# A fused S4D and channel-MLP block: token set 1 of the first half prepared one slot later, and transposed by VectorE instead of TensorE

## The chip, the cores and the metric

The program runs on one core of a Trainium2 chip. The metric is the device time of one execution in microseconds (us). One execution was also recorded by the hardware profiler; its trace gives start and length of every instruction and DMA. TensorE is called PE here, VectorE DVE, ScalarE ACT, GpSimd POOL and SyncE SP. SP does no arithmetic: it issues DMAs, in the order of its program.

## The reference, cut to what matters

```python
# u: 1 x 2048 x 576 (L tokens, D features), w1: 576 x 4608, w2: 4608 x 576
x  = u
xn = layernorm(x)
s  = S4D(xn)                     # a long convolution over the tokens for each feature, with FFTs
y  = layernorm(xn)
g  = silu(gelu(y @ w1 + b1) @ w2 + b2)
out = x + s * g
```

The change is in the MLP branch, `y @ w1`, `gelu`, `@ w2`, and in how `y` gets to it. The convolution branch is interleaved with it on all engines.

## The kernel before, in words

**Tiles.** The 2048 tokens are 16 tiles of 128 tokens, in four sets of 512 (`TB`). The first half of the program does sets 0 and 1 of the MLP (tiles 0 to 7), the second half sets 2 and 3. Within a half the hidden dimension of 4608 is taken in `NG` = 12 groups of `G` = 3 blocks of 128. A group's weights are loaded from DRAM into the ring `raw`, split into a high part (ACT, `w1h`, `w2h`) and a rest (DVE, `w1l`, `w2l`), and used by two sets. Each of these weight tiles has one buffer.

**Slots.** A slot is one group for one set `tb`: `layer1` (three blocks of 14 matmuls with 512 columns into `mxa` or `mxb`), for each block gelu and its split into `hh` (ACT) and `hl` (DVE), and `layer2` (72 matmuls with 288 columns). The sum of `layer2` over the groups is kept in `acc`; DVE adds each of the four PSUM banks to it as it is finished, with the bias `bias2` in the first group. There are 48 slots. Slot 2n is group n for the half's first set, slot 2n+1 the same group for its second.

**The input of a set.** `layer1` needs the normalized tokens with features on the partitions: `XH` and `XL` (high part and rest of the first 512 features, as four blocks `kb`) and `XR` (the last 64). Each has room for two sets. In the first half tiles of a set are normalized by `second` into a `row` tile, transposed by PE (`y_transpose`, into the PSUM tiles `cv`) and split from PSUM by ACT and DVE. This is done for set 0 at the start and for set 1 (`turn_lines`) during slot 0. For the second half `second` stores the rows to DRAM (`y_s`); `block_lines` later loads them so that blocks of 32 tokens lie on 32 partitions (36 DMAs with pieces of 128 bytes), DVE transposes 32 x 32 blocks within them (`blocks`, L1236), and ACT and DVE split the result (`high`, `low`).

**Other work.** `params` loads four small tensors by 128-byte pieces (`kt`, `pr`, `mg`, `kt` again), transposes them on DVE (L688) and computes the parameters of the convolution. `x_load` of tiles 8 to 15 (eight DMAs of 288 KB, to `w` and `v`) is one step, `rest_of_norms`. PE's convolution work uses the PSUM tiles `cv`: `kgen` (L869, 36 times), `forward` (L941), `s2` (L979), `inverse` (L1032) and `i1` (L1059). A `kgen` can run alone between MLP matmuls, or be put directly ahead of another of these units (`ride`).

**What sets the order.** Each engine runs its instructions in the order in which the program lists them, and waits at the head of its list. The class `Order` makes that list: it keeps an estimated time for each engine, takes steps from many lines of steps as their inputs become ready by that estimate, and fixes the resulting order on each engine. A DMA has no engine in it: it is a step of some length without one (`step(None, 5.5, ...)`), listed on SP's queue at the moment when the planner takes it. `END`, `ALONE` and a margin in `pe_turns` decide when PE takes convolution units, and which `kgen` runs alone. Nearly all hardware DMAs are issued by SP.

Of the kernel before, what the change touches and what calls it, by code (L numbers as in the profile page):

```python
# [212 lines left out]
def mixer_kernel(ctx, tc, u, log_a_real, a_imag, c_real, c_imag, log_dt, d_skip, w1, b1, w2, b2,  # L213
# [22 lines left out]
    y_s = dr.tile([8, P, D], F32, name="y_s")  # L236
# [114 lines left out]
    def norms(b0, n):  # L351
# [31 lines left out]
        def second(t, engine=nc.vector):  # L383
            mv, rs = MV[b0]
            y = sb.tile([P, D], F32, name="row", bufs=NROW)
            engine.tensor_scalar(y, XT[b0 + t], mv[:, t, 0:1], rs[:, 1, t:t + 1], op0=OP.subtract, op1=OP.mult)  # L386
# [45 lines left out]
    for half in range(2):  # L432
        for g in range(NG):
            PARTS += [(half, g, 1, i) for i in range(KB + 1)] + [(half, g, 2, i) for i in range(G)]
# [3 lines left out]
    def load_raw(queue=nc.sync):  # L438
# [8 lines left out]
        if which == 2:  # L447
            queue.dma_start(r, w2[(g * G + i) * P:(g * G + i + 1) * P, :])
        elif i < KB:
            queue.dma_start(r, w1[i * P:(i + 1) * P, f])  # L450
        else:
            for e in range(2):
                queue.dma_start(r[e * 64:(e + 1) * 64], w1[KB * P:, f])
# [96 lines left out]
    def layer2(g, tb, j, terms, last, alone=False):  # L550
# [5 lines left out]
        c = slice(j * P, (j + 1) * P)  # L556
        if alone and terms[0][1]:
            Q2[j] = bank2("cv")
        elif j not in Q2:
            Q2[j] = bank2(mx(j + 1))  # L560
# [9 lines left out]
        def add(dh, n):  # L570
            o = acc[:, tb * 4 + j].rearrange("p (h d) -> p h d", h=2)[:, dh:dh + n]
            b = bias2.rearrange("p (h d) -> p h d", h=2)[:, dh:dh + n]
            nc.vector.tensor_add(o, q[:, dh:dh + n, :288], b if g == 0 else o)  # L573
# [616 lines left out]
    def norm_lines(b0, n=4):  # L1190
# [6 lines left out]
        for t in range(n):  # L1197
            nl["steps"].append(step("DVE", 0.6, lambda t=t: second(t), mark=("yn", b0 + t)))
            xl["steps"].append(step("POOL", 2.6, lambda t=t: first(t), need=[("yn", b0 + t)], mark=("xs", b0 + t)))
            wx["steps"].append(step(None, 5.0, lambda: None, need=[("xs", b0 + t)], mark=("xn", b0 + t)))  # L1200

    def turn_lines(b0, tb):
        x, xh, x2 = nl, nlh, nl2
        cell = {}

        def first(k0):
            for kb in (k0, k0 + 1):
                if kb <= KB:
                    cell[kb] = y_transpose(b0, tb, kb)
                    for i in range(4):  # L1210
                        cell[kb][0](i)
        M = lambda *a: ("turn", tb, b0) + a
        for ks in ((0, 1), (2, 3), (4,)):
            x["steps"].append(step("PE", 0.5 * len(ks), lambda k0=ks[0]: first(k0), cv=1,
                                   need=[M("l", 1)] if ks[0] == KB else (), mark=M("t", ks[0])))
            for kb in ks:
                xh["steps"].append(step("ACT", 0.6, lambda kb=kb: cell[kb][1](), need=[M("t", ks[0])], mark=M("h", kb)))
            for kb in ks:
                x2["steps"].append(step("DVE", 0.6, lambda kb=kb: cell[kb][2](), cv=-(kb == ks[-1]),
                                        need=[M("h", ks[-1])], mark=("x", tb) if kb == KB else M("l", kb)))  # L1220

    YB = []

    def block_lines():

        def load(tb, kb):
            if not YB:
                YB.extend(sb.tile([P, D], F32, name="row", bufs=NROW)[:, :TB] for _ in range(4))
            y = YB[(tb + kb) % 2]
            for q in range(4 if kb < KB else 2):  # L1230
                nc.sync.dma_start(y[32 * q:32 * q + 32].rearrange("p (b j) -> p b j", j=32), dram(
                    y_s, 4 * tb * P * D + kb * P + 32 * q, [[D, 32], [32 * D, NT], [1, 32]]))

        def blocks(tb, kb):
            n, k = P if kb < KB else 64, (tb + kb) % 2
            nc.vector.transpose(YB[2 + k][:n], YB[k][:n])  # L1236

        def high(tb, kb):
            y = YB[2 + (tb + kb) % 2]
            if kb < KB:  # L1240
                nc.scalar.activation(XH[:, kb, tb], y, AF.Copy)
            else:
                nc.scalar.activation(XR[:64, tb], y[:64], AF.Copy)

        def low(tb, kb):
            y = YB[2 + (tb + kb) % 2]
            if kb < KB:
                nc.vector.tensor_sub(XL[:, kb, tb], y, XH[:, kb, tb].bitcast(F32))
            else:
                nc.vector.tensor_sub(XR[64:, tb], y[:64], XR[:64, tb].bitcast(F32))  # L1250
        ks = [(tb, kb) for tb in range(2) for kb in range(KB + 1)]
        for n, k in enumerate(ks):
            yl["steps"].append(step(None, 5.5, lambda k=k: load(*k), need=[("yt",) + ks[n - 2]] if n > 1 else (), mark=("yl",) + k))
            ml["steps"].append(step("DVE", dve(TB), lambda k=k: blocks(*k), mark=("yt",) + k,
                                    need=[("yl",) + k] + ([("y2",) + ks[n - 2]] if n > 1 else [])))
            mlh["steps"].append(step("ACT", act(TB), lambda k=k: high(*k), need=[("yt",) + k, ("free", k[0])], mark=("yh",) + k))
            ml2["steps"].append(step("DVE", dve(TB), lambda k=k: low(*k), need=[("yh",) + k], mark=("y2",) + k))
# [43 lines left out]
    turn_lines(4, 1)  # L1301
# [4 lines left out]
    nl["steps"].append(step(None, 7.0, rest_of_norms))  # L1306
# [83 lines left out]
    later(mid - 2, G - 1, lambda: x_free(0))  # L1390
# [43 lines left out]
    for slot in range(NSLOT):  # L1434
        turn[0] = slot + 1
        g, tb = slot // 2 % NG, slot % 2
        n = slot // 2
        final = slot >= NSLOT - 2
        for pos in range(NPOS):
            if pos < G:  # L1440
                need = wmark(n, 1) + [("x", tb)]
                if pos == 0:
# [4 lines left out]
                    if slot in (1, 2 * NG + 1):  # L1447
# [11 lines left out]
                if pos == G - 1 and tb == 1 and slot + 1 < NSLOT:  # L1459
                    weigh_in(1)  # L1460
            else:
# [12 lines left out]
                if last or halves:  # L1474
# [10 lines left out]
                    elif g == NG - 1:  # L1485
# [5 lines left out]
                if pos == NPOS - 1 and tb == 1 and slot + 1 < NSLOT:  # L1491
# [4 lines left out]
            pe_turns(all_lines=pos in (0, 1, G + 1, G + 4, NPOS - 1))  # L1496
# [55 lines left out]
```

## Time and profile before

| | |
|---|---|
| time, median of 3 runs (lowest, highest) | 1083.9 us (1082.99, 1084.34) |
| the profiled execution's own time | 1082.74 us |
| its span, first to last instruction | 1081.0 us |
| granted TensorE clock | 0.998 |
| busy time of DVE, ACT, POOL | 947.9, 650.7, 199.1 us |
| moved by DMA | 125.54 MB, 116 GB/s on average |

The profiled execution is 1.2 us below the median. Times of single instructions count from the start of the span. A timeline row is: start, length, engine, line, operation, output<-inputs, shapes, count, and in brackets the engine's idle time before it and what ended it. "q" behind an engine is its queue: such a row issues a DMA, and its length is that of the issue; the landing of the data is given apart. Rows of one line without a gap are merged, so that their length is that of all of them. Matmuls overlap: the distance of their starts tells their cost, not their length.

### The profile page before, as it was taken

How to read it: one execution, taken by the hardware profiler on the slowest of the kernel's cores; microseconds unless marked ns; L12 is line 12 of the kernel's file. 1: busy time of each engine (PE TensorE's matmuls, PEld its weight loads, DVE VectorE, ACT ScalarE, POOL GpSimd, SP SyncE). 2: the span in 40 equal slices, each digit the busy share in tenths (PEclk: the TensorE clock that was granted, in tenths of full speed). 3: DMA queues.
4: the chain of work that ended last, by engine and by line, in shares of the span. 5: the costliest groups of instructions: out<-in, count | busy, mean ns of one | idle time of the engine just before them, and what ended most of it. 6: DMA issues, size and time to landing. Idle time of an engine off the chain costs nothing.

```text
span 1081.0 us, 27198 instructions
## 1 busy us (share of the span) xinstructions
PE 1071.7 (99%) x11491; PEld 933.9 (86%) x11491; DVE 947.9 (88%) x1518; ACT 650.7 (60%) x974; POOL 199.1 (18%) x281
## 2 busy tenths in 40 slices
PE   9999999999999999999999999999999999999997
PEld 7989999889888888888888888888888887888896
DVE  7797878989999999999999999999999996677366
ACT  6558569767666665767756666576665754233333
POOL 6559342110000200002100010000100022110231
PEclk9999999999999999999999999999999999999999
DMA  7746455823225221455523433142312347332344
GB/s 236 229 140 190 163 186 196 229 71 113 72 71 110 65 80 55 112 94 129 144 59 100 82 86 88 33 124 55 97 53 76 115 85 237 111 111 88 89 156 117
DMA packets 136537, 125.54 MB, mean 116 GB/s; under 512 B 88156, under 2 KB 108096, under 8 KB 135392
## 3 DMA queue, kind: packets, MB, share of 16 engines
q1 hardware_dynamic: 120624, 76.44, 26.2%
q0 software_dynamic: 15040, 46.40, 13.8%
q8 instruction: 90, 1.47, 0.6%
q10 hardware_dynamic: 752, 0.97, 0.3%
q14 instruction: 31, 0.25, 0.1%
HBM read 95.52 MB, written 34.01 MB: 120 GB/s over the span
## 4 chain that ended last, share of the span: by engine, by line
PE 98%; DVE 1%; issue 1%; DMA 0%; ACT 0%; POOL 0%; ACTq 0%; POOLq 0%; DVEq 0%
PE mxa L508 22%; PE mxa L565 21%; PE mxb L565 21%; PE mxb L508 21%; PE cv L869 3%; PE cv L979 3%; PE cv L1032 2%; PE cv L941 2%; PE cv L1059 1%; DMA idp<-in_ident_dram 0%; PE mxa L523 0%; PE cv L413 0%; DVE A L646 0%; DVE row L386 0%; DVE acc L573 0%
## 5 line engine op out<-in xcount | busy, mean ns | idle before, releaser
L565 PE MATMUL mxa<-w2h,hh 128*128 128x288 f32 x573 | 171.3, 299 | 0.0
L565 PE MATMUL mxb<-w2h,hh 128*128 128x288 f32 x576 | 170.9, 297 | 0.0
L565 PE MATMUL mxb<-w2h,hl 128*128 128x288 f32 x576 | 170.0, 295 | 0.0
L565 PE MATMUL mxb<-w2l,hh 128*128 128x288 f32 x576 | 169.6, 294 | 0.0
L565 PE MATMUL mxa<-w2h,hl 128*128 128x288 f32 x573 | 169.1, 295 | 0.0
L565 PE MATMUL mxa<-w2l,hh 128*128 128x288 f32 x573 | 168.7, 294 | 0.0
L547 DVE TENSOR_TENSOR hl<-h,hh 128x512 fp32r<-128x512 f32 x144 | 99.4, 692 | 76.8 <-ACT hh L544 76.1
L541 ACT ACTIVATE h<-mxa,b1t 128x512 f32<-128x512 f32 x73 | 50.2, 690 | 126.3 <-PE mxa L508 121.7
L769 POOL DMA_DIRECT2D par<-par_s x36 | 27.3, 759 | 519.4 <-DVE mg L812 479.7
L565 PEld LDWEIGHTS mxa<-w2h,hh 128*128 128x128 f32 x573 | 107.6, 188 | 9.4 <-issue 6.3
L565 PEld LDWEIGHTS mxb<-w2h,hh 128*128 128x128 f32 x576 | 108.2, 188 | 4.9 <-issue 2.5
L565 PEld LDWEIGHTS mxb<-w2l,hh 128*128 128x128 f32 x576 | 108.1, 188 | 0.6
L565 PEld LDWEIGHTS mxa<-w2l,hh 128*128 128x128 f32 x573 | 107.6, 188 | 0.7
L565 PEld LDWEIGHTS mxb<-w2h,hl 128*128 128x128 f32 x576 | 108.1, 188 | 0.0
L565 PEld LDWEIGHTS mxa<-w2h,hl 128*128 128x128 f32 x573 | 107.5, 188 | 0.0
L541 ACT ACTIVATE h<-mxb,b1t 128x512 f32<-128x512 f32 x71 | 48.9, 689 | 76.9 <-PE mxb L508 76.1
L544 ACT ACTIVATE hh<-h 128x512 fp32r<-128x512 f32 x144 | 90.8, 632 | 4.0
L573 DVE TENSOR_TENSOR acc<-mxa,acc 128x576 f32<-128x576 f32 x88 | 65.4, 743 | 17.0 <-PE mxa L565 16.7
L508 PE MATMUL mxa<-XH,w1h 128*128 128x512 f32 x284 | 80.2, 404 | 0.0
L508 PE MATMUL mxb<-XH,w1h 128*128 128x512 f32 x280 | 77.1, 397 | 0.0
L508 PE MATMUL mxa<-XL,w1h 128*128 128x512 f32 x284 | 76.2, 390 | 0.0
L508 PE MATMUL mxa<-XH,w1l 128*128 128x512 f32 x284 | 76.0, 389 | 0.0
(231 smaller groups left out, 2420.8 us busy)
## 6 DMA issues: line engine op xcount, KB each, us to landing
raw<-in_B_w_dram SPq DMA_DIRECT2D x72, 288.0 KB, 3.3
raw<-in_B_w_dram SPq DMA_DIRECT2D x96, 192.0 KB, 2.9
par_s<-A POOLq DMA_DIRECT2D x8, 1080.0 KB, 5.9
par<-par_s POOLq DMA_DIRECT2D x36, 240.0 KB, 3.3
f2t<-f2q SPq DMA_DIRECT2D x24, 256.0 KB, 3.7
raw<-in_B_w_dram SPq DMA_DIRECT2D x48, 96.0 KB, 3.6
u_s<-in_A_u_dram POOLq DMA_DIRECT2D x16, 288.0 KB, 4.3
xc<-xn_s SPq DMA_DIRECT2D x48, 96.0 KB, 3.8
```

The costliest lines, as they stand in the source:

```text
L508: nc.tensor.matmul(q, a, b, start=j == 0, stop=j == len(ops) - 1)
L541: nc.scalar.activation(t, q, AF.Gelu_apprx_tanh, bias=b1t[:, g * G + i:g * G + i + 1], scale=1.0)
L544: LAST[0] = nc.scalar.activation(hh[:, i], t, AF.Copy)
L547: nc.vector.tensor_sub(hl[:, i], t, hh[:, i].bitcast(F32))
L565: nc.tensor.matmul(q[:, dh, :288], a[:, i, c], b[:, i, d], start=i == 0 and k == 0, stop=i == G - 1 and k == 2)
L573: nc.vector.tensor_add(o, q[:, dh:dh + n, :288], b if g == 0 else o)
L769: nc.gpsimd.dma_start(PAR[b].rearrange("p (g i) k -> p g (i k)", g=4), dram(par_s, (b // 6 * CH + b % 6 * 4) * NPAR, [[D * NPAR, P], [24 * ...
L869: nc.tensor.matmul(q[32 * g:32 * g + 32, i // 2, i % 2 * 64:i % 2 * 64 + 64], U[:, ri, 4 * g + i, :], v[:, ri, 4 * g + i, :], start=ri == ...
L941: nc.tensor.matmul(Q1ST[i, x][g // 2][64 * f:64 * f + 64, g % 2].rearrange(order), f1t[r].rearrange("p s k -> p (s k)"), rhs(r, f), start= ...
L979: nc.tensor.matmul(Q[i][32 * q:32 * q + 32, f, 2 * ri:2 * ri + 2], m[r, 4 * i + q, 32 * ri:32 * ri + 32], A2[r, 4 * p + 2 * i + q // 2, :, ...
L1032: nc.tensor.matmul(QI[q // 2][64 * f:64 * f + 64, q % 2, i], MAT["g2t", p + i // 2][r, i % 2, ri], YS[p + i // 2][0][r, i % 2, ri, f], sta ...
L1059: nc.tensor.matmul(Q[f][32 * e:32 * e + 32, t], g1t[r], A2[r, k:k + 2, 1].rearrange("p i d r -> p i r d"), start=True, stop=True, skip_gro ...
```

## The change

Slots are no longer two for each group. Slot 0 is group 0 with set 0; slots 1 to 22 are groups 1 to 11 with sets 0 and 1; slot 23 is group 0 with set 1; slots 24 and 25 are group 0 with sets 2 and 3, with the same weights; then groups 1 to 11 follow. There are 24 loads of weights as before. Set 1 is thus first used in slot 2 instead of slot 1, and group 1's weights in slot 1 instead of slot 2.

Set 1's tiles 4 to 7 are no longer transposed by PE. `second` stores them to `y_s` (now 12 tiles); SP loads them back as four blocks of 128 tokens (16 DMAs of 64 KB, pieces of 512 bytes) and one of the last 64 features (2 DMAs, pieces of 128 bytes) into parts of `A2`; DVE transposes and ACT and DVE split as in the second half. Sets 2 and 3 use the same 512-byte form. For that the features are dealt out differently: block `kb` of `XH` holds features `4*p + kb` instead of `128*kb + p`, so that the rows of `w1` are loaded with that stride, and the PE transposes of set 0 read every fourth column. The loads of tiles 8 to 15 wait until the last block of set 1 has been loaded. `END`, `ALONE`, the margin and the places where PE takes convolution units are changed, and so is the moment from which set 2's room counts as free.

```diff
-    y_s = dr.tile([8, P, D], F32, name="y_s")
+    y_s = dr.tile([12, P, D], F32, name="y_s")
...
-            if b0 >= 8:
-                nc.sync.dma_start(dram(y_s, (b0 + t - 8) * P * D, [[D, 64], [64 * D, 2], [1, D]]), y)
+            if b0 >= 4:
+                nc.sync.dma_start(dram(y_s, (b0 + t - 4) * P * D, [[D, 64], [64 * D, 2], [1, D]]), y)
...
-            nc.tensor.transpose(q[:n, i * P:(i + 1) * P], YT[b0 + i][:, kb * P:kb * P + n], idp)
+            y = YT[b0 + i]
+            y = y[:, kb:KB * P:KB] if kb < KB else y[:, KB * P:]
+            nc.tensor.transpose(q[:n, i * P:(i + 1) * P], y, idp)
...
+    SETS = [(0, (0,))] + [(g, (0, 1)) for g in range(1, NG)] + [(0, (1, 0, 1))] + [(g, (0, 1)) for g in range(1, NG)]
+    SEQ = [(n, g, tb) for n, (g, tbs) in enumerate(SETS) for tb in tbs]
+    FIRST, GATE = (0, 2, 2 * NG, 2 * NG + 1), (2 * NG - 3, 2 * NG - 1)
...
-            queue.dma_start(r, w1[i * P:(i + 1) * P, f])
+            queue.dma_start(r, dram(w1, i * F + g * G * P, [[KB * F, P], [1, n]]))
...
-    turn_lines(4, 1)
+    block_lines(0)
...
-    nl["steps"].append(step(None, 7.0, rest_of_norms))
+    nl["steps"].append(step(None, 7.0, rest_of_norms, need=[("yl0", 1, 3)]))
...
+        def source(tb, i):
+            return (0, 1, 4, 0, 5)[i] if half == 0 else (tb + i) % 2
...
+            for q in range(4 if i < KB else 2):
+                if i < KB:
+                    nc.sync.dma_start(y[32 * q:32 * q + 32].rearrange("p (b d) -> p b d", b=4), dram(
+                        y_s, (r + i) * P * D + P * q, [[D, 32], [32 * D, 4], [1, P]]))
...
+            if i < KB:
+                nc.vector.transpose(x.rearrange("p (k b t) -> p k b t", k=4, b=4),
+                                    y.rearrange("p (b j k) -> p k b j", k=4, b=4))
...
+            a["steps"].append(step(None, 3.5 + 1.5 * (k[1] == KB) if early else 5.5, lambda k=k: load(*k), mark=M("yl", *k),
+                                   need=[("ys", 4 + min(n, 3))] + ([M("yt", *ks[0])] if n == 3 else []) if early else [M("yt", *ks[n - 2])] if n > 1 else []))
...
-    END = 1020.0
-    ALONE = 3.0
+    END = 1000.0
+    ALONE = 5.0
...
-                if h is None or h[0]["eng"] != "PE" or h[1] > od.t["PE"] + (0.3 if x is nl else -0.2):
+                if h is None or h[0]["eng"] != "PE" or h[1] > od.t["PE"] + (0.3 if x is nl else -0.6):
...
-    later(mid - 2, G - 1, lambda: x_free(0))
+    later(mid - 3, G - 1, lambda: x_free(0))
...
-        g, tb = slot // 2 % NG, slot % 2
-        n = slot // 2
+        n, g, tb = SEQ[slot]
+        change = slot + 1 < NSLOT and SEQ[slot + 1][0] != n
...
-            pe_turns(all_lines=pos in (0, 1, G + 1, G + 4, NPOS - 1))
+            pe_turns(all_lines=pos in (0, 1, G + 1, G + 3, G + 5, NPOS - 1))
```

Three places show what this does to the order. Numbers behind a tile's name (`h_685`) tell uses of it apart; `A_80` is the tile `A2`.

SP's queue before, behind the second load of group 1's `w1`: the parameters `kt`, the tiles 8 to 15 (`w`, `v`), then `pr`, weights and `mg`.

```order
L681 DMA kt<-in_A_log_A_real_dram 32x18x32 x4
L264 DMA tv<-in_tvals_dram 128x32 x2
L346 DMA w<-in_A_u_dram 128x576 x6
L346 DMA v<-in_A_u_dram 128x576 x2
L681 DMA pr<-in_A_C_real_dram 32x18x32 x4
L448 DMA raw<-in_B_w_dram 128x576 x2
L681 DMA mg<-in_A_C_imag_dram 32x18x32 x4
```

The eight large loads stood ahead of `pr`. In the changed kernel SP's queue from the first stores of set 1 on reads:

```order
L388 DMA y_s<-row 64x2x576 x2
L454 DMA raw<-in_B_w_dram 128x384 x3
L388 DMA y_s<-row 64x2x576 x2
L1226 DMA A_80<-y_s 32x4x128 x8
L454 DMA raw<-in_B_w_dram 128x384
L457 DMA raw<-in_B_w_dram 64x384 x2
L1226 DMA A_80<-y_s 32x4x128 x4
L1229 DMA A_80<-y_s 32x16x32 x2
L1226 DMA A_80<-y_s 32x4x128 x4
L686 DMA pr<-in_A_C_real_dram 32x18x32 x4
L346 DMA w<-in_A_u_dram 128x576 x6
L346 DMA v<-in_A_u_dram 128x576 x2
```

Directly behind these rows stand the four loads of `mg`: the eight large loads have moved behind all of set 1's loads and behind `pr`, and stand directly ahead of `mg`.

DVE before, at the transpose of `mg` (near the end of slot 1, `hl` of `h_687` being that of slot 2's first block):

```order
L688 STREAM_TRANSPOSE A_80<-mg 128x576
L485 TENSOR_TENSOR w2l<-raw,w2h 128x576 x3
L381 RECIPROCAL U<-U 128x8
L386 TENSOR_SCALAR row<-w,U 128x576
L699 TENSOR_TENSOR kt<-kt,pr 128x576
L386 TENSOR_SCALAR row<-w,U 128x576 x3
L547 TENSOR_TENSOR hl<-h_687,hh 128x512
```

DVE in the changed kernel, at the transpose of `mg`, in slot 2 (`hl` of `h_685`, `h_712` are its first two blocks):

```order
L693 STREAM_TRANSPOSE A_80<-mg 128x576
L371 BN_STATS st<-w 128x6 x2
L373 BN_AGGR U<-st 128x2
L551 TENSOR_TENSOR hl<-h_685,hh 128x512
L371 BN_STATS st<-w 128x6
L704 TENSOR_TENSOR kt<-kt,pr 128x576
L371 BN_STATS st<-w 128x6
L373 BN_AGGR U<-st 128x2
L371 BN_STATS st<-w 128x6
L551 TENSOR_TENSOR hl<-h_712,hh 128x512
```

The statistics of tiles 8 to 10 have moved behind that transpose, among the `hl` of slot 2. A third piece of DVE's new order is set 1's own preparation, in slot 1 (`h_527` is slot 1's last block, L578 the addition to `acc`):

```order
L551 TENSOR_TENSOR hl<-h_488,hh 128x512
L1236 STREAM_TRANSPOSE A_80<-A_80 128x512 x2
L551 TENSOR_TENSOR hl<-h_527,hh 128x512
L1254 TENSOR_TENSOR XL<-A_80,XH 128x4x128 x2
L578 TENSOR_TENSOR acc<-mxb,acc 128x576
L1236 STREAM_TRANSPOSE A_80<-A_80 128x512 x2
L578 TENSOR_TENSOR acc<-mxa,acc 128x576
L1254 TENSOR_TENSOR XL<-A_80,XH 128x4x128 x2
```

The transposes have come in between `hl` and between the additions to `acc`, each of which PE waits for. On PE the 20 transposes of set 1 are gone (two rows of L413, with 16 and 4 matmuls), and of the 36 `kgen` 14 stand alone between MLP matmuls, where 21 did; the other seven are put ahead of another unit.

More of the change, by code (lines that the diff above doesn't have):

```diff
@@ L1198, in norm_lines @@
             nl["steps"].append(step("DVE", 0.6, lambda t=t: second(t), mark=("yn", b0 + t)))
+            if b0 == 4:
+                od.line()["steps"].append(step(None, 3.0, lambda: None, need=[("yn", b0 + t)], mark=("ys", b0 + t)))
             xl["steps"].append(step("POOL", 2.6, lambda t=t: first(t), need=[("yn", b0 + t)], mark=("xs", b0 + t)))
             wx["steps"].append(step(None, 5.0, lambda: None, need=[("xs", b0 + t)], mark=("xn", b0 + t)))
[L1202 to L1220, printed above, removed]
@@ L1222, in mixer_kernel, with block_lines, load @@
-    YB = []
-    def block_lines():
-        def load(tb, kb):
+    def block_lines(half=1):
+        YB = []
+        if half == 0:
+            YB += [A2F[:, k:k + TB] for k in (2 * D, PT0 + 4 * D, PT0 + 4 * D + TB, PT0 + 4 * D + 2 * TB, 0, D)]
+        M = lambda *a: a if half else (a[0] + "0",) + a[1:]
+        def source(tb, i):
+            return (0, 1, 4, 0, 5)[i] if half == 0 else (tb + i) % 2
+        def load(tb, i):
             if not YB:
                 YB.extend(sb.tile([P, D], F32, name="row", bufs=NROW)[:, :TB] for _ in range(4))
[L1229 to L1241, printed above, removed]
-            else:
[L1243 to L1251, printed above, removed]
-        for n, k in enumerate(ks):
[L1253 to L1257, printed above, removed]
@@ L1458, in mixer_kernel @@
                 od.advance(od.t["PE"])
-                if pos == G - 1 and tb == 1 and slot + 1 < NSLOT:
+                if pos == G - 1 and change:
                     weigh_in(1)
@@ L1490, in mixer_kernel @@
                     od.urgent.append((od.t["PE"], chain))
-                if pos == NPOS - 1 and tb == 1 and slot + 1 < NSLOT:
+                if pos == NPOS - 1 and change:
                     weigh_in(2)
```

44 lines of the change are left out of this document (38 added, 6 removed).

## The prediction, as put on record

> **What bounds the kernel now.** I read the engines' shares first, then busy times in stretches, then PE's, SP's and DVE's timelines from 20 to 66 us, where the change moves work. From the page and the stretches:
>
> ```profile
> PE 1071.7 (99%) x11491; PEld 933.9 (86%) x11491; DVE 947.9 (88%) x1518; ACT 650.7 (60%) x974; POOL 199.1 (18%) x281
> 34.62:1070.00 1035.38, 1035.38 (x11285) 902.10 (x11283) 914.83 (x1447) 629.49 (x932) 175.75 (x259) 1.00 0.40 113
> 446.00:535.00 89.00, 89.00 (x971) 77.38 (x970) 85.83 (x142) 61.31 (x101) 11.27 (x19) 1.00 0.52 117
> ```
>
> The columns behind the length of a stretch are the busy times of PE, PEld, DVE, ACT and POOL. From 34.62 us on PE has no idle time at all, at a clock of 1.00. So PE's list is the time: what the change takes off that list is gained, and any new wait of PE is lost one for one, since no idle time is there to take it up. DVE, at 96% where sets 2 and 3 are prepared (446 to 535 us), has little room, but PE waits for it nowhere.
>
> **What comes off PE's list.** Starts of PE's rows around set 1's transposes, and those of the next slots:
>
> ```profile
> 22.64 0.29 PE L565 MATMUL mxa<-w2h,hh 128*128 128x288 f32 x1
> 29.65 0.29 PE L565 MATMUL mxa<-w2h,hl 128*128 128x288 f32 x1
> 31.80 0.38 PE L565 MATMUL mxb<-w2h,hh 128*128 128x288 f32 x1
> 34.14 0.29 PE L565 MATMUL mxb<-w2h,hl 128*128 128x288 f32 x1
> 34.62 0.48 PE L508 MATMUL mxa<-XH,w1h 128*128 128x512 f32 x1
> 44.24 0.29 PE L565 MATMUL mxb<-w2h,hh 128*128 128x288 f32 x1
> 53.76 0.40 PE L508 MATMUL mxb<-XH,w1h 128*128 128x512 f32 x1
> ```
>
> A matmul with 288 columns costs 0.13 us from start to start (72 in the 9.52 us from 44.24 to 53.76). The 16 transposes thus cost 31.80 - 29.65 - 0.13 = 2.02 us and the four others 34.62 - 34.14 - 0.13 = 0.35; the first matmul behind each is about 0.08 longer than usual (0.38 for 0.29, 0.48 for 0.40). Their removal gains 2.5 us.
>
> The `kgen` that no longer stand alone, with one alone, an `s2` alone and a `kgen` ahead of an `s2`:
>
> ```profile
> 191.46 1.07 PE L508 MATMUL mxb<-XL,w1h 128*128 128x512 f32 x4
> 193.50 0.39 PE L508 MATMUL mxb<-XR,w1s 128*128 128x512 f32 x1
> 194.85 1.20 PE L508 MATMUL mxa<-XH,w1h 128*128 128x512 f32 x4
> 300.01 0.39 PE L508 MATMUL mxb<-XR,w1s 128*128 128x512 f32 x1
> 301.85 1.20 PE L508 MATMUL mxa<-XH,w1h 128*128 128x512 f32 x4
> 464.78 0.39 PE L508 MATMUL mxa<-XR,w1s 128*128 128x512 f32 x1
> 465.09 1.10 PE L869 MATMUL cv<-v,U 128*32 128x64 f32 x64
> 467.68 1.21 PE L508 MATMUL mxb<-XH,w1h 128*128 128x512 f32 x4
> ```
>
> Alone: 194.85 - 193.50 less one matmul (0.23) is 1.12, and the first four matmuls behind it take 0.13 more than usual (1.20 for 1.07): 1.25 us. Ahead of an `s2` it adds (467.68 - 464.78) - (301.85 - 300.01) = 1.06. Seven of them gain 7 x 0.19 = 1.3 us. Without any new wait the change gains 2.5 + 1.3 = 3.8 us.
>
> **Where set 1 and the large loads now stand.** SP's rows, the last `pr` alone with its landing, the loads from `y_s`, a window table whose last two columns are the DMA engines' share and GB/s, and DVE's addition behind slot 0's last matmul, weight splits and normalizations:
>
> ```profile
> 19.12 4.75 SPq L450 DMA_DIRECT2D raw<-in_B_w_dram  x4
> 23.92 1.13 SPq L453 DMA_DIRECT2D raw<-in_B_w_dram  x2
> 29.93 3.52 SPq L346 DMA_DIRECT2D w<-in_A_u_dram  x6
> 33.49 1.45 SPq L346 DMA_DIRECT2D v<-in_A_u_dram  x2
> 36.05 4.60 SPq L681 DMA_DIRECT2D pr<-in_A_C_real_dram  x4
> 48.35 2.65 SPq L681 DMA_DIRECT2D mg<-in_A_C_imag_dram  x4
> L681 SPq DMA_DIRECT2D pr<-in_A_C_real_dram x2: 1144/1430/1715, 37.7 to 39.5; - x2
> DMA to landing us min/median/max: 6.7/7.2/7.8
> L1231 SPq DMA_DIRECT2D row<-y_s x36: 302/488/1578, 452.7 to 529.5; - x36
> 32.00:34.00 2.00, 2.00 (x17) 2.00 (x16) 1.67 (x3) 1.27 (x3) 1.65 (x3) 1.00 0.16 54
> 34.00:36.00 2.00, 2.00 (x14) 1.78 (x13) 1.71 (x4) 1.08 (x2) 1.74 (x1) 1.00 1.01 401
> 42.00:44.00 2.00, 2.00 (x10) 1.67 (x9) 1.57 (x5) 0.62 (x1) 0.80 (x2) 1.00 1.26 255
> 34.47 0.76 DVE L573 TENSOR_TENSOR acc<-mxb,bias 128x576 f32<-128x576 f32 x1 [0.26 <-PE mxb L565]
> 55.39 2.05 DVE L485 TENSOR_TENSOR w2l<-raw,w2h 128x576 fp32r<-128x576 f32 x3
> 58.75 1.90 DVE L386 TENSOR_SCALAR row<-w,U 128x576 f32<-128x576 f32 x3
> ```
>
> *Start.* Slot 0's `layer2` begins at 22.64 and, without transposes, ends 9.52 later, at 32.2. The last addition starts 0.33 behind the last matmul's start (34.47 for 34.14), so at 32.4. The addition (0.76), four normalizations (4 x 0.63) and two weight splits (2 x 0.68) take DVE 4.6 us, to 37.0. SP then issues set 1's fourth store (0.55). Behind that stand 25 DMAs, 18 of set 1's loads, three of weights and four of `pr`. At 0.49 each (L1231's median) and a gap of 0.04 they take 13.2 us: the first of the eight large loads is issued at 50.7, not at 29.9.
>
> *`mg` behind them.* Before, `pr` stood where `mg` stands now: the last `pr` landed at 39.5 + 6.7 = 46.2, which is 16.3 us after the first large load was issued. SP issued the four slowly (4.60 us for 2.65 of `mg`'s). That gives the upper end, 50.7 + 16.3 = 67.0. For the lower end: 2.36 MB at 400 GB/s (34 to 36 us) are 5.9 us, with 2 us ahead of the first data, and `mg`, issued meanwhile, takes no more than its last DMA's usual time behind them, so 50.7 + 9.5 = 60.2. Before, data hardly flowed until 34 us (54 GB/s), behind `kt` and `tv`, and POOL's stores shared the engines later; both are missing now. But the small pieces were slow even at a full share (255 GB/s at 1.26). I take a value nearer to the lower end: 11.8 us, `mg` landed at 62.5.
>
> **Who waits for `mg`.** DVE's durations, from before:
>
> ```profile
> 54.70 0.77 DVE L688 STREAM_TRANSPOSE A<-mg 128x576 f32<-128x576 f32 x1
> 58.08 0.75 DVE L699 TENSOR_TENSOR kt<-kt,pr 128x576 f32<-128x576 f32 x1
> 60.58 0.68 DVE L547 TENSOR_TENSOR hl<-h,hh 128x512 fp32r<-128x512 f32 x1
> 61.18 0.81 DVE L371 BATCH_NORM_STATS2 st<-w 128x6 f32<-128x288 f32 x2
> 62.14 0.96 DVE L547 TENSOR_TENSOR hl<-h,hh 128x512 fp32r<-128x512 f32 x1
> ```
>
> From the transpose of `mg` to the end of slot 2's second `hl` DVE has 0.7 (transpose) + 0.96 (statistics of a tile, 61.18 to 62.14) + 0.6 + 1.5 (three half tiles, one aggregate) + 0.7 (`kt`) + 0.7 = 5.2 us. Slot 2's `layer2` would start at 32.2 + 9.52 + 2 x 9.55 = 60.8 (`layer1` takes 44.24 - 34.62 less 0.08) and needs that `hl` in its sixth matmul, at 61.4. With `mg` at 62.5 it is there at 67.7: PE stands still for 6.3 us. The sum is 6.3 - 3.8 = +2.5 us, 1082.74 + 2.5 = 1085.2 against the profiled execution. That execution lies 1.2 below the median; against the median of 1083.9 it is 1086.4.
>
> **The other waits lie inside that one.** SP's issue also delays set 1 itself. The second block's last load is issued at about 41.3 and the fourth's at 48; DVE's rows for them stand ahead of `hl` of slot 1's third block (needed at 44.4) and of the addition that frees slot 1's fourth bank (needed at 48.9). If a load lands after 2 us, PE waits some 0.3 us for the one and 2.3 for the other, 2.6 in all. They delay PE but neither SP nor `mg`, so the 6.3 us, counted against slot 2 without waits, contain them.
>
> **What I cost at nothing.** Group 1's weights are needed 21 us earlier. Their `w1` was issued from 19.1 to 25.1 us already before. DVE's last split of it now stands directly behind slot 0's third addition, which follows 54 matmuls: 22.64 + 54 x 0.13 + 0.33 + 0.76 + 0.7 = 31.5. `layer1` needs that part in its 13th matmul, near 35, so 3 us cover it. The last part of `w2` is issued behind that split and needed some 10 us later. `w1`'s other row stride leaves 128 pieces of the same size. Sets 2 and 3 have as many DMAs, transposes and splits as before; the larger pieces save DMA time that no engine waited for.
>
> **Strided reads.** PE's 20 transposes of set 0 and 12 of DVE's now read single elements 16 bytes apart; no row shows that. The nearest is a DVE transpose that reads pairs:
>
> ```profile
> L1043 DVE STREAM_TRANSPOSE A<-A x36: 667/671/715, 355.4 to 1008.1; 128x512 f32<-128x512 f32 x36
> L1236 DVE STREAM_TRANSPOSE row<-row x10: 667/694/704, 465.5 to 536.2; 128x512 f32<-128x512 f32 x8, 64x512 f32<-64x512 f32 x2
> ```
>
> Pairs (671 ns) cost no more than contiguous reads (694), so I take nothing. The other end is a doubled transpose on PE: set 0's 20 stand in the start, where PE is all there is, and would cost 2.5 us like set 1's.
> [...]
>
> **Rivals.**
> 1. *No wait for `mg`* (faster): `mg` passes the large loads, or lands before 57.5, and set 1's loads land early too. 1083.9 - 3.8 = 1080.1, up to 1081.7 with a little wait. Against it stands SP's order, and that `pr`, in the same place, landed 6.7 to 7.8 us after its issue. Chance 0.15.
> 2. *Only set 1's own waits* (no change): `mg` lands by 58.8, and the 2.6 us remain: 1082.7. Chance 0.10.
> 3. *As slow as before* (slower): `mg` takes 15 us or more from the first large load, as `pr` did. At 67.0 PE waits 10.8 us: 1090.9. For it: the only such sequence in the trace. Chance 0.10.
> 4. *Strided reads cost double* on top of the forecast: 1086.4 + 2.5 = 1088.9. Chance 0.07.
>
> **How the numbers follow.** The forecast, `mg` between 59.5 and 65 and PE waiting 3.3 to 8.8 us, has 0.58 and a range of 1083.4 to 1088.9, centre 1086.4. About 0.2%, 2.2 us, is what a measurement can tell here. The forecast is slower than that if `mg` lands after 62.2, which I give 0.33 of its 0.58, else no change. Slower: 0.33 + 0.10 + 0.07 = 0.50; same: 0.25 + 0.09 = 0.34; faster: 0.15 and 0.01 from the second rival, 0.16. The range reaches into the first and the third rival, 1081.5 to 1090.5, and leaves out most of the first and half of the third, some 0.18.
>
> **What would show it.** In the profile after: no L413-like transposes of set 1 on PE and 14 `kgen` alone (right for the gain); SP's large loads issued near 51 us and the transpose of `mg` on DVE after an idle time that ends with `mg`'s DMA near 62; PE idle in slot 2's `layer2`, ended by `hl`. PE busy throughout 40 to 75 us would make the prediction wrong, as would idle time of PE at another place, above all between 440 and 560 us, or a start of slot 0's `layer1` later than 12.96.

## The result, and the profile after

The changed kernel takes 1101.41 us (median of 5 runs, 1099.78 to 1103.3) against 1083.24 us for the kernel before beside it: ratio 1.0165, 95% interval 1.015 to 1.018, some 18 us slower. The profiled execution took 1101.41 us, with a span of 1099.6 us and a granted clock of 0.992.

Two views lead to the places: what PE waited for (total, times, longest, in us; the row ahead of them has the engines' busy times), and PE's clock in stretches of 3.41 us. Columns of the second behind the length: busy PE, PEld, DVE, ACT, POOL, then clock, DMA share and GB/s.

```profile
PE 1074.8 (98%) x11471; PEld 935.9 (85%) x11471; DVE 954.4 (87%) x1523; ACT 646.2 (59%) x969; POOL 204.9 (19%) x281
PE mxb L570 <- DVE hl L551: 11.4, 3, 4.9
PE mxa L570 <- DVE hl L551: 2.4, 2, 1.7
PE mxa L570 <- ACT h L545: 0.4, 1, 0.4
```

```profile
46.89:50.30 3.41, 0.00 (x1) 0.01 (x1) 2.69 (x4) 1.23 (x2) 1.73 (x2) 1.00 0.86 259
50.30:53.71 3.41, 3.41 (x14) 3.41 (x15) 2.92 (x4) 2.23 (x4) 0.00 (x0) 0.50 0.70 162
53.71:57.12 3.41, 3.41 (x27) 3.38 (x26) 2.51 (x4) 1.03 (x2) 0.00 (x0) 1.00 0.84 146
67.37:70.78 3.41, 2.40 (x11) 1.40 (x9) 3.31 (x10) 3.10 (x6) 0.00 (x0) 1.00 0.26 41
70.78:74.19 3.41, 2.32 (x17) 2.33 (x18) 3.38 (x8) 3.38 (x7) 0.00 (x0) 1.00 0.02 5
...
480.38:483.80 3.42, 1.56 (x9) 1.19 (x7) 3.29 (x4) 0.00 (x0) 0.00 (x0) 1.00 0.66 184
483.80:487.21 3.41, 0.31 (x2) 0.00 (x0) 3.34 (x6) 0.41 (x3) 0.00 (x0) 0.50 0.40 73
487.21:490.62 3.41, 1.94 (x8) 1.94 (x9) 3.38 (x8) 3.26 (x6) 0.00 (x0) 0.50 0.00 0
490.62:494.03 3.41, 3.41 (x56) 2.51 (x62) 3.41 (x6) 0.48 (x1) 0.00 (x0) 0.50 0.03 5
494.03:497.44 3.41, 3.41 (x46) 3.09 (x31) 2.33 (x4) 1.23 (x3) 0.00 (x0) 1.00 0.32 48
```

PE's longest waits stand at three places, always for `hl`: from 45.4 us (4.9 us, slot 1), at 70 us (1.7, slot 2) and from 481 us (1.9 and 4.6, slot 21). At the first and the third half clock follows, for one stretch and for three (of the three PE is almost idle in the first): a matmul count of 14 in a stretch where 27 fit. The first matmuls of the slots show the loss adding up, after minus before: slot 0 +0.9 us, slot 1 -1.6, slot 2 +5.1, slot 3 +8.0, slot 21 +6.9, slot 22 +16.2, the last matmul +18.7.

SP's and DVE's rows of the first half, as in the prediction's lists:

```profile
40.12 4.65 SPq L1226 DMA_DIRECT2D A<-y_s  x8
44.93 1.05 SPq L454 DMA_DIRECT2D raw<-in_B_w_dram  x1
...
50.54 2.18 SPq L1226 DMA_DIRECT2D A<-y_s  x4
52.77 2.06 SPq L686 DMA_DIRECT2D pr<-in_A_C_real_dram  x4
54.87 3.04 SPq L346 DMA_DIRECT2D w<-in_A_u_dram  x6
...
59.12 5.42 SPq L686 DMA_DIRECT2D mg<-in_A_C_imag_dram  x4
```

```profile
47.61 2.06 DVE L1236 STREAM_TRANSPOSE A<-A 128x512 f32<-128x512 f32 x2 [5.61 <-DMA A<-y_s]
49.60 0.64 DVE L551 TENSOR_TENSOR hl<-h,hh 128x512 fp32r<-128x512 f32 x1
...
54.61 1.10 DVE L1236 STREAM_TRANSPOSE A<-A 128x512 f32<-128x512 f32 x1 [1.17 <-DMA A<-y_s]
...
66.81 0.78 DVE L693 STREAM_TRANSPOSE A<-mg 128x576 f32<-128x576 f32 x1 [3.51 <-DMA mg<-in_A_C_imag_dram]
...
71.14 0.67 DVE L551 TENSOR_TENSOR hl<-h,hh 128x512 fp32r<-128x512 f32 x1
```

In slot 1 DVE stands 5.6 us at the head of its list, at the first two transposes of set 1, whose data are under way until 47.6 us; `hl` of the third block, which PE wants at 45.4, is the next instruction. In slot 2 the same happens with `mg`, 3.5 us of DVE and 1.7 of PE. And in the second half:

```profile
470.94 1.95 SPq L454 DMA_DIRECT2D raw<-in_B_w_dram  x4
472.94 1.11 SPq L457 DMA_DIRECT2D raw<-in_B_w_dram  x2
474.09 4.87 SPq L1226 DMA_DIRECT2D row<-y_s  x8
```

```profile
470.17 2.08 DVE L489 TENSOR_TENSOR w2l<-raw,w2h 128x576 fp32r<-128x576 f32 x3
478.84 1.09 DVE L1236 STREAM_TRANSPOSE row<-row 128x512 f32<-128x512 f32 x1 [6.59 <-DMA row<-y_s]
...
482.63 0.68 DVE L551 TENSOR_TENSOR hl<-h,hh 128x512 fp32r<-128x512 f32 x1
```

SP stands at six loads of `w1` until DVE has split the first block of `w2` (from 470.2) and so freed their place; set 2's loads stand behind them. Before, the first of them was issued at 452.7, 13 us ahead of its transpose; now DVE arrives at the transpose at 472.3 and waits 6.6 us. What DVE could not do meanwhile stands ahead of the third block's `hl`, which starts only at 487.9: that is PE's second wait there.

### The profile page after: what moved, and what is told of

The parts are those of the page before. It is cut to its first block, busy times and chain, and to the rows that moved or that the text cites. A ratio compares the mean times of both kernels' runs of the same rounds, so it can differ in the third digit from the quotient of the medians.

```text
span 1099.6 us, 27187 instructions
## 1 busy us (share of the span) xinstructions
PE 1074.8 (98%) x11471; PEld 935.9 (85%) x11471; DVE 954.4 (87%) x1523; ACT 646.2 (59%) x969; POOL 204.9 (19%) x281
## 4 chain that ended last, share of the span: by engine, by line
PE 86%; DVE 4%; DMA 3%; issue 2%; POOL 2%; SPq 1%; ACT 1%; DVEq 0%; ACTq 0%; POOLq 0%
PE mxb L570 19%; PE mxa L570 19%; PE mxa L512 18%; PE mxb L512 18%; PE cv L984 3%; PE cv L874 3%; PE cv L1037 2%; PE cv L946 2%; POOL w L395 1%; PE cv L1064 1%; DMA par_s<-A 1%; DVE hl L551 1%; DMA y_s<-row 1%; SPq L1226 0%; SPq L686 0%
## 5 line engine op out<-in xcount | busy, mean ns | idle before, releaser
L578 DVE TENSOR_TENSOR acc<-mxa,acc 128x576 f32<-128x576 f32 x88 | 65.7, 747 | 20.4 <-PE mxa L570 19.9
L578 DVE TENSOR_TENSOR acc<-mxb,acc 128x576 f32<-128x576 f32 x88 | 66.2, 752 | 18.3 <-PE mxb L570 17.9
L492 ACT ACTIVATE w2h<-raw 128x576 fp32r<-128x576 f32 x72 | 44.4, 675 | 60.6 <-PE mxa L570 30.3
```

The lines of the kernel that those rows point to most:

```text
L492: nc.scalar.activation(h, r, AF.Copy)
L578: nc.vector.tensor_add(o, q[:, dh:dh + n, :288], b if first else o)
```

## The experiments

The kernels below are changes of the changed kernel unless the text says otherwise. Of the first, second, sixth, seventh and ninth the list of PE's instructions is that of the changed kernel.

### 1. Set 2's first loads ahead of the w1 loads

```diff
+    later(mid - 4, NPOS - 1, lambda: block_lines(1, ((0, 0), (0, 1))))   # issues the eight DMAs, nothing else
     later(mid - 3, 0, block_lines)                                       # its first two load steps now issue nothing
```

> The changed kernel with one edit: the eight DMAs that load set 2's first two blocks are listed on SP ahead of six loads of w1 instead of behind them. The order on PE, DVE and ACT is the same. Theory: the 6.4 us of idle PE in slot 21 come from SP, which stands at those w1 loads until DVE has split w2 (470 to 472 us), so that the blocks land after DVE wants to transpose them; and the half clock from 484 to 494 us follows from that idle time. Then the eight loads are issued near 466.5 us and landed by 471, DVE does not wait at the transposes, both the idle time and the low clock in slots 21 and 22 go, and the time is 1101.4 - 9.3 = 1092 us (1091 to 1093.5). Rival 1: DVE has no room there with transposes of 1.1 us, and the wait only moves to slots 22 to 25: 1097 to 1101. Rival 2: the low clock has another cause and stays: 1101.4 - 6.4 = 1095.

Measured: 1092.98 us (1091.81 to 1094.19), 1.0094 of before (1.0079 to 1.011). The loads and DVE:

```profile
468.00 4.61 SPq L1232 DMA_DIRECT2D row<-y_s  x8
472.71 1.80 SPq L454 DMA_DIRECT2D raw<-in_B_w_dram  x4
```

```profile
473.50 2.14 DVE L1242 STREAM_TRANSPOSE row<-row 128x512 f32<-128x512 f32 x2
```

DVE's wait, PE's 6.4 us of idle time in slot 21 and the low clock behind it are all gone. The theory holds: slot 21 lasts 24.1 us instead of 33.1, by eight DMAs six places further up on SP. The whole gains a little less, 8.4 us: in the first half this run met the same waits as the changed kernel, but with two stretches more at half clock, one in slot 1 and one in slot 2 (section on the hardware).

### 2. hl of slot 1's third block ahead of the transposes

```diff
-    STREAM_TRANSPOSE A<-A x2; hl (slot 1, third block)
+    hl (slot 1, third block); STREAM_TRANSPOSE A<-A x2     # order on DVE
```

> The changed kernel with one edit: on DVE, the transposes of set 1's first two blocks stand behind hl of slot 1's third block instead of ahead of it; nothing else moves. Theory A: the 4.9 us of idle PE in slot 1 come only from these two instructions standing at the head of DVE's list until their data land (47.6 us). Then they go, with the 1.7 us of low clock behind them: 1101.4 - 6.6 = 1094.8 us. Theory B: the place in DVE's list hardly matters, since the first addition to acc stands behind the same transposes, and slot 2 needs the whole set, whose last block is issued at 50.5 to 52.7 us and lands near 54.5. Then PE waits instead for that addition (wanted near 47, made near 52.8) and slot 2 starts near 57.5 instead of 58.9: 1099.5 to 1101.5 us.

Measured: 1102.72 us (1101.8 to 1103.27), 1.0183 of before (1.0168 to 1.0199).

```profile
53.29 2.06 DVE L1252 STREAM_TRANSPOSE A<-A 128x512 f32<-128x512 f32 x2 [9.46 <-DMA A<-y_s]
```

```profile
PE mxb L570 <- DVE acc L578: 11.0, 1, 11.0
```

The wait moved from `hl` to the first addition, as theory B has it, and grew to 11.0 us. The edit did more than its text says: the fourth block is loaded into the first one's buffer, and that load now stood ahead of the transposes, so that these waited for the last block too, and read its 128 tokens in the place of the first block's. So this run does not tell what the place of `hl` alone is worth, nor how early the additions could have been; it shows that with `hl` early the addition behind the late transposes is the next thing that PE waits for.

### 3. The 512-byte form alone

The kernel before with the diff's lines for `y_transpose`, `load_raw`, `load`, `blocks`, `high` and `low` of sets 2 and 3, and no other.

> The kernel before with one part of the change alone: features dealt out as 4*p + kb, so that sets 2 and 3 are loaded in 512-byte pieces and transposed with elements 16 bytes apart, w1 rows loaded with that stride, and PE's 40 transposes of sets 0 and 1 reading every fourth column. Every engine's order is that of before. Theory: DVE's eight transposes of sets 2 and 3 take 1.1 us instead of 0.69, which DVE's other work hides, and PE's 40 transposes take up to 0.07 us more each (LDWEIGHTS 208 ns for 140): 1083.2 + 0 to 2.8 = 1084.6 us. Rival 1: the form itself made the stall of slot 21 (DVE is 96% busy there, and 8 x 0.4 us is put on it): a wait of PE between 455 and 535 us, 1086 to 1092. Rival 2: no cost anywhere: 1083.2.

Measured: 1083.45 us (10 runs, 1082.85 to 1083.92) beside 1082.67, ratio 1.0007 (0.9997 to 1.0016). PE has one wait above 0.3 us in the second half, 0.33 us at 503. The transposes:

```profile
L1244 DVE STREAM_TRANSPOSE row<-row x8: 1039/1090/1143, 466.2 to 531.3; 128x512 f32<-128x512 f32 x8
```

Elements 16 bytes apart cost DVE 1.09 us instead of 0.69. PE's 40 transposes cost 0.4 us together: from the first of set 0's to the start of slot 0 it is 3.39 us instead of 3.20 (9.96 to 13.35, 9.76 to 12.96), and set 1's 16 take 2.22 instead of 2.02. Slot 1 starts 0.6 later (35.21 instead of 34.62), but 0.2 of that is there ahead of the first transpose. Rival 1 falls: the form alone does not make the stall of slot 21.

### 4. The planning numbers alone

The kernel before with `END` 1000, `ALONE` 5.0, the margin -0.6 and the new places.

> The kernel before with the four planning numbers of the change alone (END 1000, ALONE 5.0, margin -0.6, the places where PE takes convolution units); slots, set 1's transposes on PE and the loads as before. Theory: only the kgen that no longer stand alone change PE's list, at 0.19 us each: 1082 us (1081 to 1083.2). Rival: the numbers alone move DVE's and SP's work so that a wait of PE arises: above 1085.

Measured: 1082.40 us (1081.93 to 1082.85), ratio 0.9997 (0.9987 to 1.0006): no difference, and no wait of PE above 0.5 us behind the start. The rival falls.

### 5. Set 1 on PE again, in slot 1

```diff
-    block_lines(0)
+    turn_lines(4, 1)          # on the first experiment; the large loads wait for nothing
```

> The kernel of the first experiment (set 2's first loads early), but set 1 is again transposed by PE, in slot 1: 16 transposes ahead of its third block and 4 behind it. The order of the slots, the 512-byte form for sets 2 and 3 and the planning numbers stay as changed; the large loads wait for nothing. Theory: all that is still lost against the kernel before (1093.0 - 1082.7 = 10.3 us) comes from set 1's way through DRAM and DVE: its late data in slot 1, the late mg in slot 2, and the low clock behind both. Then PE has no idle time there and the time is that of before, less 0.3 for the planning numbers, plus up to 0.8 for the strided form: 1083 us (1082 to 1084.5). Rival: the new order of the slots costs by itself, with group 1's weights needed a slot earlier: above 1086.

Measured: 1086.83 us (1084.42 to 1088.94), ratio 1.0036 (1.0025 to 1.0048): 6.2 us less than the first experiment, yet 3 to 4 more than expected, and where the rival had it. The trace shows another cause for a part:

```profile
59.17 0.78 DVE L693 STREAM_TRANSPOSE A<-mg 128x576 f32<-128x576 f32 x1 [3.98 <-DMA mg<-in_A_C_imag_dram]
```

`mg` still stands behind the eight large loads. ACT's parameter work behind it delays the gelu of slot 2, and PE waits 2.0 us. My expectation had put the late `mg` down to set 1's loads alone. Waits of 0.5 and 0.3 us for additions in the second half are a further part; for the rest this run shows no cause, and its executions lie up to 4.5 us apart. That the new order of the slots does not cost some 4 us by itself is shown by the tenth experiment, which has it and takes 1083.52.

### 6. Set 1 brought in earlier

```diff
-            return (0, 1, 4, 0, 5)[i] if half == 0 ...     # the fourth block's buffer
+            return (0, 1, 4, 6, 5)[i] if half == 0 ...     # 6: tile 4's raw input
# SP: 18 loads of set 1, w1 x3, pr, mg, large loads;  DVE: hl, transpose, addition, transpose, split, addition, ...
```

> The kernel of the first experiment with set 1 brought in earlier: its 18 loads stand on SP without the three w1 loads between them, the fourth block has a buffer of its own and so waits for no transpose, mg stands ahead of the eight large loads, and on DVE hl of slot 1's third block and the additions stand ahead of or between the transposes. PE's order is the same. Theory: the start of slot 2 is set by the landing of set 1's last block plus transpose, split and copy. The 18 loads are issued by about 49.5 us instead of 52.7 and landed by 51.5 instead of 54.5, so slot 2 starts near 54.5 instead of 58.0, and mg has landed by 58, so that slot 2 waits for nothing: 1093.0 - 3.5 - 2.0 for mg's wait - up to 2 of low clock = 1086.5 us (1085 to 1088.5). Rival: the loads are bound by the DMA engines (share 1.05 at 40 to 45 us), not by their place on SP; the last block lands as before and only mg's part is gained: 1089 to 1091.5.

Measured: 1084.83 us (10 runs, 1084.03 to 1086.64), ratio 1.0021 (1.0011 to 1.0031). In this kernel the fourth block overwrites an input that the convolution still reads, so that its output is not the reference's there. PE's waits in slot 1 and for `mg` are gone. One is left there, at the start of slot 2 (with half clock behind it), and 0.9 us in slot 22, as in the first experiment. At the start of slot 2 ACT's copy waits for DVE's transpose, and that for POOL's use of the overwritten input:

```profile
PE mxb L517 <- ACT XH L1271: 2.2, 1, 2.2
```

The theory holds, with a time 0.2 us under its range: slot 2 starts at 53.7 us instead of 58.5, so set 1's readiness set that start, and its place on SP set the readiness. `mg` and DVE's order were moved as well, so that the run does not give the share of each.

### 7. mg ahead of the large loads

```diff
# on the first experiment, order on SP:
-    x_load(8..15); mg x4
+    mg x4; x_load(8..15)
```

> The kernel of the first experiment with one more edit: mg's four loads stand on SP directly ahead of the eight large loads instead of directly behind them. PE, DVE and ACT keep their order. Theory: mg lands near 58 us instead of 66, its transpose waits for nothing, and the 1.7 and 0.3 us of idle PE in slot 2 go, with the half clock that followed them from 71.2 to 74.7 us (1.7 us lost): 1093.0 - 3.7 = 1089.3 us. Rival 1: the low clock there does not follow from so short an idle time: 1091. Rival 2: DVE's statistics of tile 8, whose load lands 2 us later, make the same wait: 1093.

Measured: 1088.17 us (1087.61 to 1088.9), ratio 1.0052 (1.0037 to 1.0067), 4.8 us less than the first experiment. SP and DVE:

```profile
55.02 2.12 SPq L690 DMA_DIRECT2D mg<-in_A_C_imag_dram  x4
57.19 2.87 SPq L346 DMA_DIRECT2D w<-in_A_u_dram  x6
```

```profile
63.12 0.78 DVE L699 STREAM_TRANSPOSE A<-mg 128x576 f32<-128x576 f32 x1
```

No wait ahead of the transpose, no idle time of PE in slot 2, and no half clock there. Behind the wait of slot 1 stands one stretch at half clock where the first experiment had two, which would account for the saving being larger than expected.

### 8. Waits of set sizes in the kernel before

```diff
+    STALL = {3: 4, 4: 5, 5: 6, 6: 7, 7: 8, 8: 10, 9: 12}     # slot: extra computations of hl of its third block
```

> The kernel before, with hl of the third block computed 4, 5, 6, 7, 8, 10 and 12 times more in slots 3 to 9, at about 0.6 us each, so that PE idles once in each of these slots, from about 1 to 6 us. It measures what an idle time does to the granted clock. Theory A: the clock is judged in fixed stretches of about 3.4 us; a stretch in which PE stands still for most of the time is followed by half clock for one stretch or more, so that idle times under some 1.5 us cost nothing more, those of 4 us and above always cost a further 1.7 us or more, and those between do or don't, by where they fall. Theory B: any idle time above a fixed length, between 1.7 and 4.6 us, gives half clock for the same length of time each.

Measured, in one execution of 1131.64 us: PE idles once in each slot, for 3.0, 3.2, 3.9, 4.6, 5.4, 6.8 and 8.3 us. Half clock follows for 1, 1, 2, 1, 2, 2 and 3 stretches of 3.41 us. Slots 3, 5 and 6 (idle 3.0, 3.9 and 4.6 us):

```profile
84.94:88.35 3.41, 0.37 (x4) 0.15 (x2) 3.31 (x5) 3.35 (x6) 3.06 (x3) 1.00 0.26 96
88.35:91.76 3.41, 3.41 (x15) 3.41 (x16) 3.36 (x6) 3.36 (x4) 3.06 (x3) 0.51 0.48 97
91.76:95.18 3.42, 3.42 (x28) 3.42 (x27) 2.97 (x4) 1.44 (x2) 3.12 (x5) 0.99 0.87 333
...
132.72:136.14 3.42, 0.40 (x4) 0.17 (x2) 3.28 (x5) 2.51 (x4) 1.98 (x4) 1.00 0.97 342
136.14:139.55 3.41, 2.53 (x10) 2.54 (x11) 3.36 (x8) 0.00 (x0) 0.53 (x1) 0.51 0.24 72
139.55:142.96 3.41, 3.41 (x16) 3.41 (x16) 2.21 (x4) 0.00 (x0) 0.00 (x0) 0.50 0.64 210
...
160.03:163.44 3.41, 0.00 (x0) 0.00 (x0) 3.27 (x5) 1.04 (x2) 0.00 (x0) 1.00 0.04 10
163.44:166.86 3.42, 3.21 (x13) 3.21 (x14) 3.13 (x5) 0.39 (x1) 0.00 (x0) 0.51 0.00 0
166.86:170.27 3.41, 3.41 (x28) 3.41 (x27) 2.33 (x6) 1.72 (x2) 1.11 (x2) 0.99 0.02 5
```

Theory A holds for the idle times that were made here, 3.0 us and more; its 3.4 us are seen in the changed kernel too, whose half clock lasts 3.41 us from 50.30 and three times as long from 483.80. Of shorter ones 0.9 us left the clock at 1.00 (seventh experiment, at 502 us), and 2 us did so in the changed kernel and not in the first experiment (section on the hardware). All seven low times begin and end on one grid of 3.413 us, and their number does not follow the length of the idle time (3.9 us gave two, 4.6 us one) but how that falls into the grid.

### 9. The sixth with a free buffer

```diff
+                if i == 3:
+                    YB.append(sb.tile([P, D], F32, name="row", bufs=NROW)[:, :TB])      # source 6
```

> The sixth experiment with another buffer for set 1's fourth block: a row tile, which is free by then, instead of the place of tile 4's raw input, which the convolution still needed. Nothing else moves. Theory: DVE's 2.0 us of waiting for POOL ahead of that block's transpose goes, with it the 2.25 us of idle PE at the start of slot 2 and the half clock behind it (55.2 to 58.8 us, 1.8 us lost): 1084.8 - 4.0 = 1080.8 us (1080 to 1082), so the gain that was forecast without waits is there once the waits are gone. Rival: the last block's landing binds as well, a wait of 1 to 2 us stays, with half clock behind it: 1082.5 to 1084.5.

Measured: 1085.09 us (11 runs, 1083.88 to 1085.44), ratio 1.0011 (1.0002 to 1.002). The time lies above both ranges; the rival's is the nearer.

```profile
46.64 1.08 DVE L1259 STREAM_TRANSPOSE A<-A 128x512 f32<-128x512 f32 x1 [2.47 <-DMA A<-y_s]
```

```profile
PE mxb L575 <- DVE acc L583: 1.8, 2, 1.6
...
PE mxa L575 <- DVE hl L556: 0.9, 1, 0.9
PE mxb L517 <- ACT XH L1273: 0.6, 1, 0.6
PE mxb L517 <- DVE XR L1277: 0.5, 1, 0.5
```

The wait at the start of slot 2 shrank to 0.6 and the half clock went. But in this profiled execution the first block landed at 46.5 us instead of 44.0 in the sixth, and the first addition, behind its transpose, made PE wait 1.6 us. The edit does not move that block. In the tenth kernel, where SP has set 1's loads in the same order, it landed at 44.8, and the wait is 0.3 us:

```profile
44.99 1.09 DVE L1259 STREAM_TRANSPOSE A<-A 128x512 f32<-128x512 f32 x1 [1.18 <-DMA A<-y_s]
```

So the landing differs from one execution to another by about as much as this wait. How much of the 1.6 us is in the ninth kernel's median is not shown.

### 10. Transposes planned at their measured length

```diff
-            b["steps"].append(step("DVE", dve(TB), ...
+            b["steps"].append(step("DVE", dve(TB) if early else 1.1, ...      # on the ninth
```

> The same kernel with one number of the plan: for the second half DVE's transposes are planned at 1.1 us, as measured, instead of 0.6. That moves convolution work from slot 21 on. Theory: the 0.9 us of idle PE in slot 22, where hl stands behind two strided transposes, goes: 0.9 less than the kernel beside it. Rival: the plan's later order brings other waits, and the time is the same or up to 2 us more.

Measured: 1083.52 us (11 runs, 1082.18 to 1084.53) beside 1083.18, ratio 1.0001 (0.9992 to 1.0009), 1.6 less than the ninth. PE's wait of 0.9 us in slot 22 is gone, as the theory has it; what made the other 0.7 us is not shown. The traces can't tell: the tenth's execution is the lowest of its eleven and the ninth's the highest. This is the best form of the change that was run: as fast as the kernel before, not faster. PE still waits for set 1 three times, for 0.3, 0.5 and 0.6 us.

The repairs against the kernel before, each beside its own runs of it:

| kernel | us over before | taken away |
|---|---|---|
| changed | 18.2 | |
| 1: set 2's loads early | 10.3 | 7.9 us: slot 21 and its half clock |
| 7: and mg ahead of the large loads | 5.5 | 4.8 us: slot 2 and its half clock, one stretch less in slot 1 |
| 9: and set 1 earlier | 1.9 | 3.6 us: slot 1 and its half clock |
| 10: and the plan's length | 0.3 | 1.6 us: 0.9 of it the wait in slot 22 |

A row is not the price of its wait alone: how much half clock follows a wait changes with the moment at which it falls, and earlier repairs move that moment.

## Why the prediction was wrong, by its steps

**The gain: right for the transposes, half as large for kgen.** Slot 0 is 2.48 us shorter (forecast 2.5). The convolution units take 131.3 us of PE in the ninth kernel against 132.0 before (sum of the distances between the MLP matmuls around them, less one matmul): 0.7 us for the forecast 1.3. The 1.06 us that a `kgen` adds ahead of an `s2` was read rightly. A `kgen` ahead of a `forward` or an `i1` adds 1.03 us against 1.12 alone; the 0.13 us behind a lone one, which I counted as saved, are paid behind the other unit as well.

**What I cost at nothing: this is the step that failed.** "Sets 2 and 3 have as many DMAs, transposes and splits as before" is true and did not matter. I counted them and did not look at where they stand on SP. `block_lines` is listed at the same slot number, but slot 21 was the second slot of its group and is now the first: the six `w1` loads that wait for DVE's splits of `w2` come ahead of set 2's loads instead of behind. The term that was put at nothing measured 9.0 us in slot 21, its half clock included (33.1 us in the changed kernel, 24.1 in the first experiment); its repair took 7.9 of the 18.2 us away. The prediction named PE idle between 440 and 560 us as what would make it wrong, and it did.

**The other waits "inside" the one for mg: the wrong way round.** I took 2 us from issue to landing, though the profile before has a median of 3.2 us for the second half's loads from `y_s` (1.9 to 5.2), and got 2.6 us of wait in slot 1. The first eight of set 1's loads landed 3.7 to 5.4 us after their issue while the DMA engines were fully shared (1.07 in 40 to 45 us); only the last four took 2.0 to 2.6. The transposes stood at the head of DVE's list, and slot 1 became 6.7 us longer. Slot 2 then began at 58.9 us, not at 51.3, and so most of the wait for `mg` lay inside the waits of slot 1.

**mg: mechanism right, size off.** It landed 11.8 us after the first large load's issue (66.68 - 54.87), just as estimated, which is in part luck, as the value was picked between 9.5 and 16.3. But that load was issued at 54.87 us, not at 50.7: set 1's last store was issued at 38.9 us instead of 37.0, the first load 0.7 us behind the store's end, and the 25 DMAs took 14.8 us instead of 13.2. PE waited 1.7 + 0.4 us for `mg` instead of 6.3, because slot 2 was late itself. Taking that wait away from the first experiment was worth 4.8 us, half clock included.

**The clock: missing.** No step of the sum had the granted clock in it; a new wait was to be "lost one for one". Four stretches of 3.41 us at half clock belong to the waits of slots 1 and 21. Where PE had work in them, they come on top of the waits.

**Strided reads: little on the path, but not nothing.** I took the pairs of L1043 as the nearest row. Of set 0's 20 transposes on PE 16 are strided; the four of the last 64 features are not. DVE's transposes of single elements 16 bytes apart take 1.09 us against 0.69 for contiguous reads and 0.67 for those pairs, so the row for pairs did not tell what single elements cost. For PE the other end, 2.5 us, was far too much: 0.2 us for set 0's. Slot 0's `layer1` did start later than 12.96, at 13.84, a sign that I had named; but 0.7 of it is a later first transpose (10.45 instead of 9.76), for which PE waited 1.2 us for the DMA of `idp` instead of 0.55. In the first experiment, with the same reads, that wait is missing and slot 0 starts at 12.92. DVE's 0.4 us each is hidden in the third experiment and may be part of the 0.9 us of wait in slot 22 of the ninth.

**The rivals.** The sign, slower, was the likeliest of the three, but that it came out is for the larger part luck: of the 18.2 us the repair of `mg` gave back 4.8. The four rivals were about set 1, `mg` and the form; none was about the second half or the clock.

## What to carry to other kernels

Before an edit of the order is costed at nothing, find each moved DMA's new place on its queue and what the entries ahead of it wait for; equal counts say nothing. An instruction that waits for a DMA at the head of an engine's list holds up all that stands behind it, as the transposes of slot 1 did with `hl` for 5.6 us of DVE and 4.9 of PE; so list it by the landing that is measured under load (3.7 to 5.4 us here), not by a quiet one (2.0 to 2.6). Where PE has no idle time, a wait of a few microseconds can cost nearly double, because half clock can follow it: 2.0 us in slot 2 of the first experiment cost some 1.7 more, estimated from the 3.41 us at clock 0.50 behind them, with 13 matmuls where 28 fit.

## What the runs showed of the hardware that I had not expected

The granted clock changed on a fixed grid. In the eighth experiment seven low times, from 88 to 252 us, start at multiples of 3.413 us from one another (0, 7, 14, 22, 29, 37 and 45 stretches behind the first), and in the changed kernel 50.30 and 483.80 lie 127 stretches apart. In all cases but one PE's busy time in a stretch told whether half clock followed it. Where low times give the place of the grid, stretches behind the start at full clock with 1.72 us of work (second experiment), 1.90 and 2.3 us (changed kernel) were not followed by half clock, and those with 1.61 us or less were, except this one in the seventh:

```profile
43.09:46.50 3.41, 1.55 (x12) 1.32 (x10) 0.23 (x1) 0.31 (x1) 3.06 (x3) 1.00 1.03 346
```

Half clock came there only one stretch later, behind 0.39 us, so that busy time alone does not decide it; what else enters is open. At half clock a stretch with 2.53 us of work did not end it (eighth experiment, from 136.14), and stretches with 3.19 (first, from 71.16) and 3.21 us (eighth, from 163.44) did. So an idle time of 2 us cost nothing more or some 1.7 us more, by where it fell; the 1.7 is an estimate, half of one stretch. The changed kernel and the first experiment have the same wait in slot 2: in the one it is cut by the grid (2.40 and 2.32 us busy, clock 1.00, shown above), in the other not:

```profile
67.75:71.16 3.41, 1.61 (x7) 0.73 (x5) 3.31 (x9) 3.35 (x8) 0.00 (x0) 1.00 0.00 0
71.16:74.57 3.41, 3.19 (x13) 3.19 (x14) 2.70 (x7) 3.38 (x7) 0.00 (x0) 0.50 0.06 13
```

A stretch that half clock followed was not always idle throughout: PE worked for 1.61 us in the one from 67.75, and for 1.54 us in the eighth experiment's from 238.54.
